# One pass over four tiles for the first unit's feed-forward, on weights still in SBUF; attention on four tokens at once

## The chip, the cores and the metric

The kernel runs on one core of one Trainium2 chip. The metric is the device time of one launch in microseconds (us), median of the runs. Names of the engines in the rows: PE is TensorE's matmuls, PEld its weight loads, DVE is VectorE, ACT is ScalarE, POOL is GpSimd, and SP is SyncE, which here issues all the transfers.

## The reference

2,048 tokens of 640 channels go through two layers of the same two blocks, with the same weights in both:

```python
def A(x):      # 32 heads of 20 channels, a window of 8 keys at distances 0, 2, ... 14
    q, k, v = split(layernorm(x) @ wqkv)               # 640 x 1920
    logits = sum(q * k[pos - 2*w], over 20 channels) * 20**-0.5    # masked where pos < 2*w
    return (softmax(logits, over the 8 keys) @ v[pos - 2*w]) @ wo
def B(x):      # per token, 640 -> 1536 -> 640
    return gelu(layernorm(x) @ w1 + b1) @ w2 + b2
x = x + A(x); x = x + B(layernorm(x)); x = x + A(x); x = x + B(layernorm(x))
```

## The kernel before, in words

The tokens are cut into four units of 512 (even and odd positions, two halves of each), and a unit into four tiles (`t`) of 128. A layer and a unit make a step `n` = 0 to 7. Matmuls run in float16 on operands that are split into a high part and the rest, three products for each (`PASS`), so every weight is also split once: ACT writes the scaled high part (L475), DVE the rest (L476).

For each step: `layernorm` ("a"), `qkv` (L648, in 16 pieces of 15 matmuls), whose results go through ACT (`ev`) to memory (`spill`), from which q, k and v come back with the window of the keys laid out (`fetch`, L690). `attention` works on DVE, for a quarter of the heads (a group `G`, 32 in all): products q by k (L732), their sums over 20 channels (L736), softmax (L741 to L751), weights by v (L758) and a tree of additions over the 8 keys (L766, L770). It takes the four tokens of a partition two at a time (`EH = 2`), so each of these instructions stands twice, with 2,560 elements per partition. The last group's rest (L780, on DVE) lets the DMA transposes go that feed `project` (L805, wo); then `layernorm` ("b") and DMA transposes (L620, `yT`).

`mlp` is the feed-forward. Its 12 blocks `e` each have inner matmuls (L871, weights `c1`, 15 of them), gelu and high part on ACT (L877, L880; `hhi`), the rest on DVE (L882; `hlo`) and outer matmuls (L892, weights `c2`; two passes need `hhi`, the third `hlo`). `PARTS` lists the passes: unit 0 of the first layer in two halves of two tiles (256 columns to an inner matmul), the next five steps in one pass of four tiles (512 columns); the last two steps are done together by `pair()`.

The weights of the feed-forward (24 blocks of 320 KB) are loaded to a staging buffer (L501), split, and the split pair is sent to memory (`mw`, L517); every pass of `mlp`, unit 0's too, loads its blocks from there (L864) into the slots `c1` and `c2`, three of each. Unit 0's first inner matmul waits until all 24 blocks and wo have been split (`split_done`).

The order on every engine is set ahead of time by `Plan.run`, which places the operations by priority in a modelled time and emits them; on the chip each engine takes its instructions in that order. SP's queue is such an order too: a transfer that waits holds all that stand behind it. DVE instructions named in `PAIRS` are those that share a port with POOL.

## Time and profile before

| | us |
|---|---|
| time, median of 3 runs (1144.21 to 1144.93) | 1144.45 |
| span of the profiled execution, first to last instruction | 1146.1 |
| PE's last matmul starts at | 1142.36 |
| PE busy | 1137.1 (99%) |
| DVE busy | 1038.4 (91%) |
| ACT busy | 606.6 (53%) |

The profiled execution has no time of its own beside its span; the span is 1.65 us above the median of the runs. A busy PE is one with a matmul in its pipe. Whether the matmuls also follow one another at full rate is seen from the starts in the timeline.

### The profile page before, as it was taken

The page shows a single profiled execution, that of the slowest core. Times are in us where ns is not written, and L with a number is a line of the kernel's source. Part 1 is how long each engine was busy: PE and PEld are TensorE (multiplying, and loading weights), DVE is VectorE, ACT ScalarE, POOL GpSimd, SP SyncE. Part 2 cuts the span into 40 slices and gives each one's busy share as a digit, 9 for nine tenths or more (in the row PEclk, how much of TensorE's full clock was granted, in tenths as well). Part 3 has the DMA queues.
Part 4 walks back from the last instruction along what each step waited for, and adds up shares of the span by engine and source line. Part 5 has one row for each costly group of instructions (what it writes and reads, how often), then busy time and mean ns, then how long its engine had stood idle before and what let it go on. Part 6 is the DMA issues. An engine that isn't in the chain of part 4 may idle for free.

```text
span 1146.1 us, 17470 instructions
## 1 busy us (share of the span) xinstructions
PE 1137.1 (99%) x6812; PEld 628.4 (55%) x6812; DVE 1038.4 (91%) x1028; ACT 606.6 (53%) x1131; POOL 113.2 (10%) x94
## 2 busy tenths in 40 slices
PE   9999999999999999999999999999999999999998
PEld 6444446567565465546555555556455556555476
DVE  7999999999899999999999999999999993847972
ACT  6485336536365275734537662479347445657720
POOL 1010000211111102110112012012111000000000
PEclk9999999999999999999999999999999999999999
DMA  9999998978976477576655965569686555974201
GB/s 318 307 299 266 329 302 244 321 264 244 239 189 232 140 221 213 178 207 198 186 187 176 221 190 164 175 188 192 164 247 183 175 171 156 217 239 122 65 24 69
DMA packets 239791, 235.47 MB, mean 205 GB/s; under 512 B 139020, under 2 KB 195164, under 8 KB 239708
## 3 DMA queue, kind: packets, MB, share of 16 engines
q1 hardware_dynamic: 239708, 234.36, 69.9%
q8 instruction: 53, 0.87, 0.3%
q14 instruction: 30, 0.25, 0.1%
HBM read 157.55 MB, written 44.78 MB: 177 GB/s over the span
## 4 chain that ended last, share of the span: by engine, by line
PE 72%; DVE 3%; DMA 1%; issue 0%; ACT 0%; DVEq 0%
PE acc L892 18%; PE ps L871 17%; PE ps L648 17%; PE ps L805 10%; PE acc L1073 4%; PE ps L1108 3%; PE ps L1073 2%; DMA yT<-w 1%; DVE yT L1020 1%; DVE pr L1005 1%; PE acc L1108 1%; DVE wq L1194 0%; DVE wq L1182 0%; DVE v L1195 0%; DVE xf L1196 0%
## 5 line engine op out<-in xcount | busy, mean ns | idle before, releaser
L648 PE MATMUL ps<-wq,yT 128*128 128x480 f16 (+1 forms) x1950 | 391.0, 363 | 1.5 <-DMA yT<-w 1.1
L648 PEld LDWEIGHTS <-yT 128*128 128x128 f16 x1950 | 189.3, 98 | 200.8 <-DMA yT<-w 1.4
L892 PE MATMUL acc<-c,act 128*128 128x512 f16 (+1 forms) x1728 | 249.3, 299 | 2.3 <-DMA c<-mw 1.6
L871 PE MATMUL ps<-yT,c 128*128 128x512 f16 (+1 forms) x1260 | 247.8, 350 | 0.0
L892 PEld LDWEIGHTS <-act 128*128 128x128 f16 x1728 | 136.1, 98 | 108.8 <-issue 1.9
L871 PEld LDWEIGHTS <-c 128*128 128x128 f16 x1260 | 120.9, 98 | 107.3 <-DMA c<-mw 0.3
L732 DVE TENSOR_TENSOR pr<-qk 128x2560 f32<-128x2560 f32 x64 | 179.5, 2808 | 0.0
L758 DVE TENSOR_TENSOR pr<-sm,v 128x2560 f32<-128x2560 f32 x64 | 179.1, 2818 | 0.3
L736 DVE TENSOR_REDUCE sm<-pr 128x128 f32<-128x2560 f32 x64 | 179.2, 2801 | 0.0
L665 ACT ACTIVATE ev<-ps 128x480 f32<-128x480 f32 x128 | 72.6, 568 | 177.2 <-PE ps L648 157.5
L877 ACT ACTIVATE act<-ps,b 128x512 f32<-128x512 f32 (+1 forms) x84 | 52.4, 624 | 172.9 <-PE ps L871 170.2
L766 DVE TENSOR_TENSOR pr<-pr 128x640 f32<-128x640 f32 (+1 forms) x128 | 143.1, 1150 | 0.3
L805 PE MATMUL ps<-wo,yT 128*128 128x320 f16 x960 | 131.7, 299 | 0.0
L805 PEld LDWEIGHTS <-yT 128*128 128x128 f16 x960 | 93.8, 98 | 37.4
L780 POOL TENSOR_TENSOR ohl<-w,ohl 128x640 f16<-128x640 f32 x24 | 34.9, 1456 | 425.9 <-DVE pr L732 171.6
L882 DVE TENSOR_TENSOR act<-act 128x512 f16<-128x512 f32 (+1 forms) x84 | 51.0, 609 | 16.0 <-ACT act L880 15.9
L587 POOL TENSOR_TENSOR ln<-ln,half 128x2 f32<-128x2 f32 (+1 forms) x31 | 36.2, 1173 | 276.6 <-ACT ln L584 276.6
L625 POOL TENSOR_TENSOR xf<-xf,b 128x640 f32<-128x640 f32 x24 | 37.3, 1558 | 144.6 <-DVE pr L732 58.4
L880 ACT ACTIVATE act<-act 128x512 f16<-128x512 f32 (+1 forms) x84 | 47.5, 565 | 3.4 <-PE acc L892 1.5
L610 ACT ACTIVATE w<-xf,ln 128x640 f32<-128x640 f32 x53 | 47.5, 909 | 2.7 <-DVE w L618 2.1
L570 ACT ACTIVATE junk<-xf 128x640 f16<-128x640 f32 x57 | 41.8, 733 | 12.9 <-DVE xf L814 8.0
L618 DVE TENSOR_TENSOR w<-w,w 128x640 f16<-128x640 f32 x56 | 45.7, 830 | 2.1 <-ACT w L616 2.1
(200 smaller groups left out, 984.1 us busy)
## 6 DMA issues: line engine op xcount, KB each, us to landing
c<-mw SPq DMA_DIRECT2D x174, 320.0 KB, 3.6
spill<-ev SPq DMA_DIRECT2D x64, 480.0 KB, 3.6
qk<-spill SPq DMA_DIRECT2D x32, 880.0 KB, 6.0
v<-spill SPq DMA_DIRECT2D x32, 880.0 KB, 5.3
qk<-spill SPq DMA_DIRECT2D x32, 320.0 KB, 3.6
act<-in_B_w_dram SPq DMA_DIRECT2D x24, 320.0 KB, 4.9
mw<-c SPq DMA_DIRECT2D x24, 320.0 KB, 4.7
pr<-in_B_w_dram SPq DMA_DIRECT2D x24, 320.0 KB, 4.1
```

The source lines that it names most:

```text
L648: nc.tensor.matmul(ps, transposed(yk)[:, a * KD + k, t * P:(t + 1) * P], wq[:, b, k, g, i0:i1], start=first and j == 0, stop=last and j == ...
L665: act(3 * GC, -400 + n, lambda i=i, pk=pk, ek=ek: nc.scalar.activation(tile_of(*ek)[:, :, i], tile_of(*pk)[:, :3 * GC].rearrange("p (a c) ...
L732: nc.vector.tensor_mul(tile_of(*pk), w[:, HALO + m + t0:HALO + m + t0 + EH, None, :].to_broadcast([P, EH, W, GC]), windows(w, t0, [GC, W], ...
L736: dve(E, G - 0.7, lambda pk=pk, t0=t0: nc.vector.tensor_reduce(lg(t0, t0 + EH).rearrange("p t w h -> p (t w h)"), tile_of(*pk).rearrange(" ...
L758: nc.vector.tensor_mul(tile_of(*vk).rearrange("p t w (h d) -> p t (w h) d", d=DH), lg(t0, t0 + EH).rearrange("p t w h -> p t (w h)")[:, :, ...
L766: dve(EH * w * GC, G - 0.9, lambda vk=vk, w=w: nc.vector.tensor_add(tile_of(*vk)[:, :, 0:w], tile_of(*vk)[:, :, 0:w], tile_of(*vk)[:, :, w ...
L805: nc.tensor.matmul(tile_of(*pk)[:, :D // 2], transposed(yk)[:, a * KD + k, t * P:(t + 1) * P], wo[:, b, k, c * D // 2:(c + 1) * D // 2], s ...
L871: nc.tensor.matmul(tile_of(*pk)[:, :nt], tile_of(*ck)[:, a, k * P:(k + 1) * P], transposed(yk)[:, c * KD + k, t0 * P:t1 * P], start=i == 0 ...
L877: act(nt, -430, lambda pk=pk, h32=h32, e=e: nc.scalar.activation(tile_of(*h32)[:, :nt], tile_of(*pk)[:, :nt], AF.Gelu_apprx_tanh, bias=b1[ ...
L882: dve(nt, -1000, lambda h32=h32, hk=hk: nc.vector.tensor_sub(tile_of(*hk)[:, 1, :nt], tile_of(*h32)[:, :nt], tile_of(*hk)[:, 0, :nt]), nee ...
L892: nc.tensor.matmul(accs[k][:, c0:c0 + n], tile_of(*hk)[:, a, (i - t0) * P:(i - t0 + 1) * P], tile_of(*wk)[:, c, w0:w0 + n], start=first, s ...
L1073: nc.tensor.matmul(tile_of(*to(i))[:, :HALF], hl()[:, a, i * P:(i + 1) * P], row(c), start=start and (a, c) == PASS[0], stop=(a, c) == PAS ...
```

## The change

Four things go together. `PARTS` gives unit 0 one pass over four tiles. That pass takes its weights from the slot in which the split wrote them (keys `("prep", e)`); the store to `mw` stays, for the later passes. The raw weights are loaded into slots of `c1` and `c2` too, so a raw block, its split pair and the blocks in use share three slots; the loads come where the pass needs them (priority -252, was 10), and no inner matmul waits for all splits. `attention` takes four tokens in one instruction (5,120 elements), and the logits lie with the 8 keys of a head next to each other (before, 8 heads apart). The first-layer `qkv` of unit 3 gets a late priority, so that it fills in.

```diff
-PARTS = [(0, 0, 2), (0, 2, 4)] + [(b, 0, 4) for b in range(1, 2 * NU - 2)]
+PARTS = [(b, 0, 4) for b in range(2 * NU - 2)]
...
     def prep_m(f, i, prio):
         ck = (f"c{i + 1}", ("prep", f))
...
-        prep_rows(("m", f, i), prio, src, lambda: tile_of(*ck)[:, 0], lambda: tile_of(*ck)[:, 1], [ck])
-        dma(328, prio - 5, lambda: nc.sync.dma_start(mw[i][f], tile_of(*ck)),
+        prep_rows(("m", f, i), (f"c{i + 1}", ("raw", f)), prio, src, lambda: tile_of(*ck)[:, 0], lambda: tile_of(*ck)[:, 1], [ck], -180)
+        dma(328, prio - 1, lambda: nc.sync.dma_start(mw[i][f], tile_of(*ck)),
...
-                prio, done = -500 + n + 0.01 * k, ("qkvp", n, t, g)
+                prio, done = (-500 if n != NU - 1 else 13) + n + 0.01 * k, ("qkvp", n, t, g)
...
-            dve(E, G - 0.6, qk, need=[("inq", G), ("ink", G)], give=[("qk", G, a)], use=[wk, pk, sk])
-            dve(E, G - 0.7, lambda pk=pk, t0=t0: nc.vector.tensor_reduce(
-                lg(t0, t0 + EH).rearrange("p t w h -> p (t w h)"), tile_of(*pk).rearrange("p t w (h d) -> p (t w h) d", d=DH),
-                axis=AX.X, op=OP.add), need=[("qk", G, a)], give=[("lg", G, a)], use=[pk, sk])
+        dve(E, G - 0.6, qk, need=[("inq", G), ("ink", G)], give=[("qk", G)], use=[wk, *pk, sk])
+        dve(E, G - 0.7, lambda: nc.vector.tensor_reduce(by_key(), heads(), axis=AX.X, op=OP.add),
+            need=[("qk", G)], give=[("lg", G)], use=[*pk, sk])
...
+        dve(E, G - 0.85, lambda: nc.vector.tensor_mul(
+            heads(), by_key()[:, :, :, None].to_broadcast([P, W, m * GH, DH]), windows(tile_of(*vw), [DH, m * GH], [1, DH])),
+            need=[("at", G), ("inv", G)], give=[("pv", G)], use=[vw, sk, *vk])
...
-            ck, wk = ("c1", j), ("c2", j)
-            for i, k in enumerate((ck, wk)):
+            ck, wk = (("c1", j), ("c2", j)) if at else (("c1", ("prep", e)), ("c2", ("prep", e)))
+            cgot, wgot = ([k] if at else [("lo", ("m", e, i))] for i, k in enumerate((ck, wk)))
+            for i, k in enumerate((ck, wk) if at else ()):
                 dma(328, -250 + j + 1.5 * i, lambda k=k, i=i, e=e: nc.sync.dma_start(tile_of(*k), mw[i][e]),
...
-            mm(3 * KD * nt, 15, j - 1.0 - AHEAD, inner, need=[*ready, ck, *split_done] + [("hhi", j - 2)] * (e > 1), give=[("hp", j)],
+            mm(3 * KD * nt, 15, j - 1.0 - AHEAD, inner, need=[*ready, *cgot] + [("hhi", j - 2)] * (e > 1), give=[("hp", j)],
...
-            prep_m(f, i, 10 + f)
+            prep_m(f, i, -252 + f)
```

Where it moves instructions, at three places. On PE, where unit 0's first inner matmuls end (`c_79` and `c_77` to `c_76` are slots of `c1`, `c_80` and `c_81` of `c2`, `yT_74` is unit 0's input). Before, the second block's inner matmuls are followed by outer ones:

```order
L871 MATMUL ps_95<-yT_74,c_79 128x256
L892 LDWEIGHTS act
L892 MATMUL acc_97<-c_81,act 128x512
...
L871 LDWEIGHTS c_80
L871 MATMUL ps_94<-yT_74,c_80 128x256
```

With the change the inner matmuls have 512 columns, and a piece of unit 3's `qkv` (15 matmuls) stands between them and the outer ones:

```order
L851 MATMUL ps_92<-yT_74,c_76 128x512
L639 LDWEIGHTS yT_72
L639 MATMUL ps_94<-wq,yT_72 128x480
...
L872 LDWEIGHTS act
L872 MATMUL acc_96<-c_80,act 128x512
```

All that stands ahead of it moved too: wo of unit 0 comes after 30 of unit 3's qkv matmuls (before, after 120), then 135 more of them, then the first inner matmuls. Of unit 3's last 75, 15 stand here and 60 after block 4's inner matmuls.

On DVE, around the second `hlo` of unit 0 (L882, now L862), before: two short instructions together, between attention's halves, and no split left to do:

```order
L758 TENSOR_TENSOR pr_77<-sm_90,v_68 128x2560
L882 TENSOR_TENSOR act<-act 128x256 x2
L766 TENSOR_TENSOR pr_77<-pr_77 128x2x640
L882 TENSOR_TENSOR act<-act 128x256
L766 TENSOR_TENSOR pr_77<-pr_77 128x2x320
```

With the change, from group 7's q by k on (L722); L466 is the split's rest, `c11<-c12` writes slot 1 of `c1` from the raw block in slot 2:

```order
L722 TENSOR_TENSOR pr_95<-qk0_67 128x5120
L862 TENSOR_TENSOR act_66<-act_66 128x512
L740 RECIPROCAL sm0_87<-sm0_87 128x32
L727 TENSOR_REDUCE sm1_88<-pr_95 128x8x32
L862 TENSOR_TENSOR act_66<-act_66 128x512
L466 SCALAR_TENSOR_TENSOR c11_77<-c12_78,c11_77 128x640
L466 SCALAR_TENSOR_TENSOR c21_80<-c22_81,c21_80 128x640
L466 SCALAR_TENSOR_TENSOR c12_78<-c10_76,c12_78 128x640
```

The splits of blocks 2 and 3 now stand behind the second `hlo`, between attention's long instructions; those of blocks 0 and 1 come much earlier, and blocks 4 to 11 follow in the same way.

On SP's queue, in the same stretch, before: loads of split blocks.

```order
L690 DMA v0_68<-spill00_135 128x1760
L864 DMA c22_83<-mw14_127 128x1280
L864 DMA c10_78<-mw06_117 128x1280
L864 DMA c11_79<-mw07_118 128x1280
L864 DMA c20_81<-mw15_128 128x1280
```

With the change: raw loads (L492) in turn with the stores of split blocks (L508), in one queue with attention's v (L681).

```order
L508 DMA mw03_113<-c12_78 128x1280
L492 DMA c10_76<-in_B_w1_dram 128x5x128
L681 DMA v0_68<-spill00_134 128x1760
L492 DMA c12_78<-in_B_w1_dram 128x5x128
L508 DMA mw13_125<-c20_79 128x1280
L492 DMA c22_81<-in_B_w2_dram 128x640
```

A raw load now waits until its slot's last reader is done, and the split of the block that it brings waits for the load.

## Rows read from the trace of the kernel before

**Rows 1.** Windows: length; busy us of PE, PEld, DVE, ACT, POOL; PEclk; DMA.

```profile
180.00:345.00 165.00, 161.58 (x1123) 104.61 (x1121) 158.64 (x147) 86.17 (x178) 22.67 (x16) 0.99 0.87 251
240.00:260.00 20.00, 20.00 (x153) 14.38 (x153) 19.17 (x17) 4.65 (x11) 2.43 (x2) 0.91 0.73 239
345.00:1140.00 795.00, 794.94 (x4722) 431.24 (x4721) 713.86 (x708) 423.74 (x770) 76.86 (x55) 1.00 0.61 176
```

**Rows 2.** Timeline of PE, 180 to 292: start, us, instruction, [idle before, releaser].

```profile
180.69 16.46 PE L805 MATMUL ps<-wo,yT 128*128 128x320 f16 x120
...
221.29 3.44 PE L871 MATMUL ps<-yT,c 128*128 128x256 f16 x30
...
237.99 0.72 PE L892 MATMUL acc<-c,act 128*128 128x512 f16 x4 [0.73 <-DVE act L882]
239.97 1.05 PE L892 MATMUL acc<-c,act 128*128 128x512 f16 x4 [1.26 <-DMA c<-mw]
240.81 3.16 PE L871 MATMUL ps<-yT,c 128*128 128x256 f16 x15
243.81 1.25 PE L892 MATMUL acc<-c,act 128*128 128x512 f16 x8
...
251.43 1.80 PE L871 MATMUL ps<-yT,c 128*128 128x256 f16 x15
253.07 1.79 PE L892 MATMUL acc<-c,act 128*128 128x512 f16 x12
...
289.52 0.70 PE L892 MATMUL acc<-c,act 128*128 128x512 f16 x4 [0.35 <-DMA c<-mw]
291.30 12.32 PE L648 MATMUL ps<-wq,yT 128*128 128x480 f16 x60 [1.07 <-DMA yT<-w]
```

**Rows 3.** The chain that ended last, in order of time: start, us, what.

```profile
303.62 16.30 PE ps L805 x120
319.92 12.15 PE ps L648 x60
...
399.73 3.26 PE acc L892 x24
402.99 3.24 PE ps L871 x15
```

**Rows 4.** Groups of instructions by line and form: count, busy us, mean ns of one.

```profile
L758 DVE TENSOR_TENSOR pr<-sm,v 128x2560 f32<-128x2560 f32 x64 | 179.1, 2818 | 0.3
L766 DVE TENSOR_TENSOR pr<-pr 128x1280 f32<-128x1280 f32 x64 | 93.8, 1483 | 0.1
L877 ACT ACTIVATE act<-ps,b 128x512 f32<-128x512 f32 x60 | 41.1, 685 | 137.6 <-PE ps L871 134.9 <-DVE pr L766 2.3
L749 DVE TENSOR_REDUCE sm<-sm 128x32 f32<-128x256 f32 x32 | 19.5, 611 | 6.3 <-ACT sm L747 6.2
L476 DVE SCALAR_TENSOR_TENSOR c<-act,c 128x640 f16<-128x640 f32 x24 | 19.1, 820 | 3.5 <-ACT c L475 3.5
L475 ACT ACTIVATE c<-act 128x640 f16<-128x640 f32 x24 | 16.8, 727 | 0.8 <-DMA act<-in_B_w_dram 0.8
L745 DVE TENSOR_TENSOR sm<-sm 128x256 f32<-128x256 f32 x32 | 13.4, 420 | 0.3
```

**Rows 5.** Timeline of DVE: start, us, instruction.

```profile
40.15 2.82 DVE L732 TENSOR_TENSOR pr<-qk 128x2560 f32<-128x2560 f32 x1
...
66.11 5.55 DVE L732 TENSOR_TENSOR pr<-qk 128x2560 f32<-128x2560 f32 x2
71.58 2.81 DVE L736 TENSOR_REDUCE sm<-pr 128x128 f32<-128x2560 f32 x1
...
226.02 0.76 DVE L882 TENSOR_TENSOR act<-act 128x256 f16<-128x256 f32 x2
```

**Rows 6.** Line L501 alone (weight loads): time to landing.

```profile
DMA to landing us min/median/max: 3.2/4.8/6.9
```

**Rows 7.** Line L587 alone (POOL's power in layernorm): duration ns min/median/max.

```profile
L587 POOL TENSOR_TENSOR ln<-ln,half x31: 547/706/3451, 12.8 to 980.6; 128x2 f32<-128x2 f32 x26, 128x1 f32<-128x1 f32 x5
```

More of the change, by code (lines that the diff above doesn't have):

```diff
@@ L356, in transposed @@
         return tile_of(*key).rearrange("p (k c) -> p k c", k=2 * KD)
-    blocks = [("o", k) for k in range(KD)] + [("m", f, i) for f in range(NF) for i in range(2)]
-    through = {name: next(pool for pool, n in THROUGH if i < n) for i, name in enumerate(blocks)}
-    split_done = [("lo", k) for k in blocks]
-    def passed(pool):
-        return [("lo", k) for k in blocks if through[k] == pool]
     wq = sb.tile([P, 2, KD, NG, 3, GC], HT, name="wq")
@@ L504, in prep_rows @@
             packet=4 * P if name[0] == "m" and not name[2] else 4 * D)
-        a, v = split(hi, lo, lambda: tile_of(*key))
-        act(D, prio, a, need=[("st", name)], give=[("hi", name)], use=[key, *use])
-        dve(D, next(p for n, p in LOP if blocks.index(name) < n), v, need=[("hi", name)], give=[("lo", name)], use=[key, *use])
+        a, v = split(hi, lo, raw)
+        act(D, prio + first, a, need=[("st", name)], give=[("hi", name)], use=[key, *use])
+        dve(D, LOP, v, need=[("hi", name)], give=[("lo", name)], use=[key, *use])
     def prep_o(k, prio):
-        prep_rows(("o", k), prio, lambda: A_wo[k * P:(k + 1) * P], lambda: wo[:, 0, k], lambda: wo[:, 1, k])
+        prep_rows(("o", k), ("sa", ("o", k)), prio, lambda: A_wo[k * P:(k + 1) * P], lambda: wo[:, 0, k], lambda: wo[:, 1, k])
     def prep_m(f, i, prio):
@@ L739, in attention, with heads, qk @@
-        last = [("lg", G, a) for a in range(NE)]
+        def heads():
+            return pr.rearrange("p w t (h d) -> p w (t h) d", d=DH)
+        pk, vk = ([("pr", (G, j, i)) for i in range(2)] for j in range(2))
+        def qk():
+            w = tile_of(*wk)
+            nc.vector.tensor_mul(pr.rearrange("p w t c -> p w (t c)"),
+                                 w[:, HALO + m:HALO + 2 * m].rearrange("p t c -> p (t c)")[:, None, :].to_broadcast([P, W, m * GC]),
+                                 windows(w, [1, m * GC]))
@@ L774, in hi @@
+        last = ("pv", G)
+        for w in (4, 2):
+            dve(m * w * GC, G - 0.9, lambda w=w: nc.vector.tensor_add(pr[:, 0:w], pr[:, 0:w], pr[:, w:2 * w]),
+                need=[last], give=[("ad", G, w)], use=vk)
+            last = ("ad", G, w)
+        dve(m * GC, G - 0.9, lambda: nc.vector.tensor_add(ot(), pr[:, 0], pr[:, 1]), need=[last], give=[("o", G)], use=[*vk, ok])
         def hi():
@@ L777, in attention @@
         act(m * GC, -350 + G, lambda: nc.scalar.activation(hi(), ot(), AF.Copy),
-            need=[("o", G, a) for a in range(NE)], give=[("oh", G)], use=[ok, hk])
+            need=[("o", G)], give=[("oh", G)], use=[ok, hk])
         def lo(eng):
@@ L782, in attention @@
         if g < NG - 1:
[L783 removed]
+            pool(ASIDE, -300 + G, lambda: lo(nc.gpsimd), need=[("oh", G), ("qk", G + 1)], give=[("ol", G)], use=[ok, hk],
                  pair=True)
```

88 lines of the change are left out of this document (30 added, 58 removed).

## The prediction

> **What bounds the kernel now.** I read the windows first. From 345 to 1140 us PE is busy for 794.94 of 795.00 us at the full granted clock [rows 1]; a stretch with a matmul in the pipe all the time can still hide slow matmuls, so the starts matter: in the chain, 24 outer matmuls take 3.26 us, 15 inner ones 3.24, 60 of qkv 12.15 and wo's 120 take 16.30, one behind the other, with PE before PE [rows 3]. There the kernel is a row of matmuls, and nothing that frees DVE, ACT or DMA moves the end. What can be won lies earlier: the window from 180 to 345 has 161.58 busy of 165.00, and 240 to 260 was granted 0.91 of the clock [rows 1]. PE's timeline shows the places [rows 2]: all four waits with a releaser lie between 237 and 292, which is unit 0's feed-forward. They are 0.73 us for its `hlo` on DVE, 1.26 and 0.35 for weights that come from memory, and 1.07 for the transposes of a layernorm ahead of qkv.
>
> **What the change removes.** (1) The four waits: 0.73 + 1.26 + 0.35 + 1.07 = 3.41 us. (2) Behind the first two the clock fell to its lower level, 1.2 GHz: the 15 inner matmuls from 240.81 to the next group at 243.81 took 3.00 us, while later 15 such took 253.07 - 251.43 = 1.64; the four outer ones ahead took 0.84 (239.97 to 240.81) where 24 take 3.26, so 0.54 [rows 2, 3]. That is 1.36 + 0.30 = 1.66. The wait of 1.07 at 291 had no such sequel. (3) Unit 0's inner matmuls: 24 groups of 15 with 256 columns at 1.64 against 12 groups with 512 at 3.24, 39.36 - 38.88 = 0.48 [rows 2, 3]. The columns are the same, the number of matmuls halves. All else on PE keeps its count. So 5.55 us can be won, and no more.
>
> **What it adds on PE: can the new pass be fed?** Its order has 90 fewer qkv matmuls ahead of unit 0's wo, 90 x 0.2025 = 18.2 us, so wo starts at 180.69 - 18.2 = 162.5. Then wo 16.3, 135 of qkv 27.3: the first inner matmul at 206.1 instead of 221.29. Two inner groups (6.5), 15 of qkv (3.0), the outer matmuls of block 0 (3.3) and the first two passes of block 1 (16 of 24, 2.2) bring PE to 221.1, where it wants the second `hlo`.
>
> On DVE the order has 98 instructions from the first q by k to that `hlo`. One of 2,560 elements takes 2.82 us and one of 1,280 takes 1.48 [rows 4], so 0.15 is fixed, and 5,120 make 5.49 alone; two of 2,560 start 5.47 apart together and overlap by 0.08 [rows 5], which makes 5.40 from start to start. So 22 long ones are 118.9, the six of 2,560 and six of 1,280 are 25.4, 25 of 640 at 0.75 are 18.9, 39 short ones at about 0.35 are 13.6: 176.8. The same sum for before, over the 144 instructions from 40.15 to the first `hlo` at 226.02, gives 179.2 where 185.9 passed [rows 5]: 6.7 idle, of which 3.5 were waits for ACT's part of the splits [rows 4], which the change puts elsewhere. One more split stands ahead of the first q by k (0.82). So 40.15 + 0.8 + 176.8 + 3.2 = 221.0, and the `hlo` is there at 221.7: PE waits 0.6, or 0 to 4 with none or all of the 6.7 idle and the unseen cost of the new layout.
>
> Next, block 4. Its raw load can go when block 3 is split, three splits behind that `hlo`, at 223.9. It lands after 4.8 (3.2 to 6.9) [rows 6], ACT takes 0.73, DVE 0.82 [rows 4], with 0.4 for issue and hand-over: 230.7, and a long instruction that has just begun on DVE adds up to 5.4. PE wants it at 222.5 + two inner groups 6.5 + outer matmuls 4.1 = 233.1. So 0 to 3 us late. The queue holds a store of a split block, attention's v and the next raw load behind one another; where the split is late, those are too, and v is what DVE asks for next.
>
> These delays don't add: PE that has waited once is later for all that follows, so the pass costs the largest delay, not their sum. I take 1.5 for it, nearer to the two estimates than to their ends, and 0.5 for the 1.07 before qkv, a chain of layernorm and transposes, which the change moves and doesn't remove: 2.0, with 0 and 6.5 as ends (4 for the `hlo`, 0.8 for a load at its longest beyond that, 1.7 for a second fall of the clock).
>
> **What it changes on DVE, at nothing.** Six pairs in each of 32 groups become one instruction: 192 x 0.15 = 29 us of busy time less. The sums over 8 keys read neighbours instead of elements 32 bytes apart: 0.61 us against 0.42 for a plain instruction of 256 [rows 4], 64 x 0.19 = 12 less. The stride moves into one long write and one long read, whose cost no row shows: 0 to 12 us in all. The cover is PE's unbroken row. What could uncover it is the longer instruction ahead of an `hlo`: from the end of an inner group to the third outer pass PE has 3.26 + 3.24 + 2.17 = 8.7 us of other work; gelu, high part and `hlo` take up to 0.69 each [rows 4], with hand-overs 2.4. That leaves 6.3, so one long instruction (5.4) hides, two don't. The 48 loads of split weights that go (24 blocks, two half passes) free DMA time that nothing waits for after 345.
>
> The port is a rule that speaks against long instructions. POOL's power in layernorm takes 0.55 us at the least and 3.45 at the most, one DVE instruction of 2,560 longer [rows 7]. The Trainium skill, "SBUF — State Buffer", section "SBUF: two separate sides", says that VectorE with two SBUF inputs and GpSimd hold a shared port for a whole instruction, and that the other one is fully blocked; by it the longest power here would be 6.1. The trace agrees as far as it goes. In this kernel the last tile of layernorm "b" of unit 0 would come 2.7 later by a power behind a long instruction and 2.7 by its own DVE step behind another, 5.4; between the end of wo and the first inner matmul there were 221.29 - (180.69 + 16.3) = 24.3 us [rows 2, 3] and are 27.3. So 2.4 late at worst.
>
> **The sum.** Against the profiled execution: 1146.1 - 3.41 - 1.66 - 0.48 + 2.0 = 1142.5 us of span, 3.6 less. That execution is 1.65 above the median of the runs, and 0.31% less of 1144.45 is 1140.9.
>
> **The rivals.** *New waits take the place of the old.* If `hlo` or the split blocks make PE wait for 3.3 to 7.9 us, the time is within 0.2% of before, which is about what a measurement of this kernel can tell. For it speaks that every block of the pass now hangs on a load, ACT, DVE and a slot in turn, and that two waits together brought the clock down before; against it, the filler of 75 qkv matmuls and wo of unit 1 among the blocks. About 1143.8. *POOL is held.* The layernorm 2.4 late: 1143.3. For it the longest row, against it the 3.0 us of added room. *The split's own cycle becomes the bound, and the kernel slower.* From inner block 2 to inner block 11 PE has nine inner groups (29.2), about as much of outer ones (28.6), 60 of qkv (12.2) and wo (16.3): 86.3 us, 9.6 for a block. A block's cycle is 4.8 + 0.73 + 0.82 + 0.4 = 6.75, and with a whole long DVE instruction in front each time 12.2: nine times 2.6 more, so 1144.45 - 5.5 + 23 = 1162. With half of one it is 9.4 and costs nothing; from 10.2 on it eats the gain, from 10.5 on it decides. Against it: a load may run while the block before it is in use, and the order puts two or three splits together. *Nothing is lost:* all waits go and none come, 1138.9.
>
> **How the numbers follow.** Forecast, new waits under 3.3 us (with the case of none, 0.12): 0.62, and all of it faster by more than 0.2%. New waits 0.15 and POOL 0.08: the same, 0.23. The cycle, with anything else that costs more than 7.9: 0.15, slower. The range goes from 1138.5 (nothing lost, and 0.4 for the runs' spread) to 1145.2 (waits of 6.3); about 0.05 lies below it and 0.14 above.
>
> **What will show it.** PE in the windows between 200 and 345: idle under 3 us, no stretch below the full clock, and inner groups of 512 at 3.24 in a row. The second `hlo` at 220 to 224, and PE's wait for it under 1 us. Waits for loads of `c` from `mw` gone in unit 0, at most one or two for L466. DVE near 1000 us busy, its long instructions at 5.4 to 5.5. The forecast is wrong if PE shows waits on split weights that return block after block, if the clock falls in the new pass, or if waits come up after 345, where there were none.

## The result, and the profile after

The changed kernel takes 1147.38 us (median of 10 runs, 1146.71 to 1148.25), the kernel before in the same sitting 1144.38 (10 runs, 1144.16 to 1146.83): a ratio of 1.0023, 95% interval 1.0014 to 1.0032. It is slower by about 0.2%; forecast were 1140.9 us, within 1138.5 to 1145.2.

The two traces seem to say the opposite: the changed kernel's span is 1145.2 us, and that of the first trace of before was 1146.1. Where a run's time and its span are both known, the time is 1.7 to 1.9 longer (here 1146.95 against 1145.2). So the first trace of before is of an execution that takes some 1147.9, longer than any of the ten runs of before; of all 128 runs of before on record three are as long (1148.32 to 1148.92). This decides half of the case, below.

The changed kernel's windows, with the columns of [rows 1]:

```profile
160.00:180.00 20.00, 18.53 (x131) 12.47 (x129) 19.93 (x11) 14.01 (x36) 1.14 (x2) 1.00 0.79 185
180.00:345.00 165.00, 162.67 (x941) 84.61 (x940) 162.36 (x121) 90.40 (x163) 28.63 (x18) 1.00 0.74 216
240.00:260.00 20.00, 20.00 (x103) 9.58 (x102) 19.74 (x13) 8.57 (x15) 1.69 (x1) 1.00 0.70 229
345.00:1140.00 795.00, 794.81 (x4702) 430.89 (x4701) 696.19 (x564) 413.72 (x755) 90.24 (x52) 1.00 0.61 173
```

From 345 us on PE is as busy as before. Up to there it idles 2.33 us between 180 and 345, and 1.47 ahead of 180, where before had no wait. DVE is busy for 162.36 of 165, which leaves it next to no room. The clock is full. PE's timeline, as in [rows 2]:

```profile
164.34 16.47 PE L784 MATMUL ps<-wo,yT 128*128 128x320 f16 x120 [1.47 <-DMA yT<-ohl]
...
207.98 6.64 PE L851 MATMUL ps<-yT,c 128*128 128x512 f16 x30
214.46 3.20 PE L639 MATMUL ps<-wq,yT 128*128 128x480 f16 x15
217.50 5.60 PE L872 MATMUL acc<-c,act 128*128 128x512 f16 x40
223.49 0.99 PE L872 MATMUL acc<-c,act 128*128 128x512 f16 x6 [0.40 <-DVE act L862]
224.32 6.64 PE L851 MATMUL ps<-yT,c 128*128 128x512 f16 x30
...
285.03 4.24 PE L784 MATMUL ps<-wo,yT 128*128 128x320 f16 x30 [0.18 <-DVE xf L793]
...
316.60 6.64 PE L851 MATMUL ps<-yT,c 128*128 128x512 f16 x30 [1.34 <-DMA yT<-w]
...
323.70 3.36 PE L872 MATMUL acc<-c,act 128*128 128x128 f16 x23 [0.41 <-DVE c L466]
```

Five waits, 3.80 us: wo of unit 0 for its transposes, the second `hlo`, wo of unit 1, unit 1's first inner matmul for the transposes of its layernorm, and the last block's split. After each wait some 0.17 us more are lost, in which the pipe fills: 30 inner matmuls in a row show 6.64 busy, but the next group starts 6.47 after their start.

Two stretches of other engines show what stands ahead of the first two waits. DVE where wo's input is finished (`ohl`, L759), and SP's queue beside it:

```profile
150.04 5.49 DVE L722 TENSOR_TENSOR pr<-qk 128x5120 f32<-128x5120 f32 x1
155.45 0.82 DVE L759 TENSOR_TENSOR ohl<-w,ohl 128x640 f16<-128x640 f32 x1
```

```profile
155.56 0.81 SPq L681 DMA_DIRECT2D qk<-spill  x2
156.48 9.91 SPq L772 DMA_TRANSPOSE yT<-ohl  x4
```

And DVE around the two `hlo` (L862), with ACT's high part (L860) that the second one needs:

```profile
211.15 5.48 DVE L722 TENSOR_TENSOR pr<-qk 128x5120 f32<-128x5120 f32 x1
216.55 0.68 DVE L862 TENSOR_TENSOR act<-act 128x512 f16<-128x512 f32 x1
217.15 0.35 DVE L740 RECIPROCAL sm<-sm 128x32 f32<-128x32 f32 x1
217.41 5.43 DVE L727 TENSOR_REDUCE sm<-pr 128x256 f32<-128x5120 f32 x1
222.76 0.68 DVE L862 TENSOR_TENSOR act<-act 128x512 f16<-128x512 f32 x1
223.35 2.44 DVE L466 SCALAR_TENSOR_TENSOR c<-c,c 128x640 f16<-128x640 f32 x3
```

```profile
215.57 0.63 ACT L860 ACTIVATE act<-act 128x512 f16<-128x512 f32 x1
```

ACT is done at 216.20, 1.2 us before DVE begins a 5.43-us sum, but in DVE's order the 0.68-us instruction stands behind that sum. The same at 150: ACT's high part of `ohl` is done at 150.78, and the rest of it runs behind the long q by k, 4.7 us later.

### The profile page after: what moved, and what is told of

It reads as the page before. It is cut to its first block, busy times and chain, and to the rows that moved or that the text cites. A ratio compares the mean times of both kernels' runs of the same rounds, so it can differ in the third digit from the quotient of the medians.

```text
span 1145.2 us, 16770 instructions
## 1 busy us (share of the span) xinstructions
PE 1135.2 (99%) x6632; PEld 609.9 (53%) x6632; DVE 1026.9 (90%) x823; ACT 600.3 (52%) x1107; POOL 140.2 (12%) x94
## 4 chain that ended last, share of the span: by engine, by line
PE 74%; DVE 19%; issue 5%; DMA 2%; ACT 1%; SPq 0%; DVEq 0%; ACTq 0%
PE ps L639 24%; PE acc L872 16%; PE ps L851 15%; PE ps L784 9%; DVE sm L727 4%; PE acc L1053 4%; PE ps L1088 3%; DVE pr L743 3%; DVE pr L748 3%; DVE pr L722 3%; PE ps L1053 2%; DMA b<-in_B_b_dram 1%; DVE pr L985 1%; DVE yT L1000 1%; DVE c L466 1%
## 5 line engine op out<-in xcount | busy, mean ns | idle before, releaser
L851 PE MATMUL ps<-yT,c 128*128 128x512 f16 x1080 | 243.4, 379 | 1.3 <-DMA yT<-w 1.3
L722 DVE TENSOR_TENSOR pr<-qk 128x5120 f32<-128x5120 f32 x32 | 175.4, 5480 | 21.0 <-DMA qk<-spill 20.7
L743 DVE TENSOR_TENSOR pr<-sm,v 128x5120 f32<-128x5120 f32 x32 | 177.7, 5554 | 0.4
L727 DVE TENSOR_REDUCE sm<-pr 128x256 f32<-128x5120 f32 x32 | 175.2, 5476 | 0.0
L851 PEld LDWEIGHTS <-c 128*128 128x128 f16 x1080 | 103.4, 98 | 122.2 <-issue 1.5
L748 DVE TENSOR_TENSOR pr<-pr 128x2560 f32<-128x2560 f32 x64 | 143.1, 2236 | 0.5
L857 ACT ACTIVATE act<-ps,b 128x512 f32<-128x512 f32 x72 | 49.2, 683 | 126.5 <-PE ps L851 126.2
L759 POOL TENSOR_TENSOR ohl<-w,ohl 128x640 f16<-128x640 f32 x24 | 48.6, 2026 | 346.4 <-DVE pr L743 151.8
L862 DVE TENSOR_TENSOR act<-act 128x512 f16<-128x512 f32 x72 | 49.8, 695 | 6.7 <-ACT act L860 6.5
L756 ACT ACTIVATE ohl<-w 128x640 f16<-128x640 f32 x32 | 23.5, 734 | 49.1 <-DVE w L751 49.0
L860 ACT ACTIVATE act<-act 128x512 f16<-128x512 f32 x72 | 45.0, 626 | 4.3 <-PE acc L872 2.9
```

Of the source, the lines that this page charges most:

```text
L722: nc.vector.tensor_mul(pr.rearrange("p w t c -> p w (t c)"), w[:, HALO + m:HALO + 2 * m].rearrange("p t c -> p (t c)")[:, None, :].to_broa ...
L727: dve(E, G - 0.7, lambda: nc.vector.tensor_reduce(by_key(), heads(), axis=AX.X, op=OP.add), need=[("qk", G)], give=[("lg", G)], use=[*pk, sk])
L743: dve(E, G - 0.85, lambda: nc.vector.tensor_mul(heads(), by_key()[:, :, :, None].to_broadcast([P, W, m * GH, DH]), windows(tile_of(*vw), [ ...
L748: dve(m * w * GC, G - 0.9, lambda w=w: nc.vector.tensor_add(pr[:, 0:w], pr[:, 0:w], pr[:, w:2 * w]), need=[last], give=[("ad", G, w)], use=vk)
L851: nc.tensor.matmul(tile_of(*pk)[:, :nt], tile_of(*ck)[:, a, k * P:(k + 1) * P], transposed(yk)[:, c * KD + k, t0 * P:t1 * P], start=i == 0 ...
L862: dve(nt, -1000, lambda h32=h32, hk=hk: nc.vector.tensor_sub(tile_of(*hk)[:, 1, :nt], tile_of(*h32)[:, :nt], tile_of(*hk)[:, 0, :nt]), nee ...
```

## The experiments

Times are medians, each with its ratio to runs of before on the same chip (95% interval). Before was itself 0.2 to 1.2 us longer in the later sittings, so the kernels are compared by ratio: 0.001 is 1.1 us, and the changed kernel has 1.0023. The letters (A, E, G and so on) are the theories named in the expected texts.

**1. The kernel before, again** (no edit).

> The kernel before, unchanged, for a second trace. Theory A (the execution shown in the first trace, 1146.1 us of span, was a slow one of its kind, and my sum was made against the wrong start): in the changed kernel every run is 1.75 us longer than its span (1146.95 against 1145.2), so an ordinary execution of before has a span of 1144.4 - 1.75 = 1142.6; this trace shows 1142.3 to 1143.2, with the clock at its full level between 240 and 260 and less than 2 us of waits in unit 0's feed-forward instead of 3.41. Rival B (that execution is ordinary, a profiled run of before is just longer than its timed ones): 1145.5 to 1146.5 again, with the same four waits and the fall of the clock. Time under both: ratio 1.000, within 0.001.

1144.96 us, 1.0003 (0.9995 to 1.0012); span 1143.2 for a run of 1144.96. PE's timeline has these waits and no others from 10 us on:

```profile
238.64 1.26 PE L892 MATMUL acc<-c,act 128*128 128x512 f16 x8 [0.69 <-DVE act L882]
...
269.70 3.20 PE L892 MATMUL acc<-c,act 128*128 128x128 f16 x23 [0.71 <-DVE xf L936]
...
288.42 12.32 PE L648 MATMUL ps<-wq,yT 128*128 128x480 f16 x60 [0.27 <-DMA yT<-w]
```

1.67 us instead of the 3.41 of [rows 2]; neither wait for weights from memory, and no fall of the clock (1.00 between 240 and 260). A holds. The first trace showed a real execution, but not an ordinary one: the 1.26-us wait for weights and the lower clock behind it are in that execution and not in this one.

From this trace the account closes. PE's last matmul starts at 1139.48 in it and at 1141.48 in the changed kernel, 2.00 later. The terms: waits 3.80 - 1.67 = 2.13; two more refills of the pipe, 0.34; fewer matmuls, -0.48; an earlier start (the first qkv of 480 columns at 16.89 instead of 17.31), -0.42; a late outer matmul at 619.40, 0.29. That is 1.86. It is the account of these two executions, whose times are 1.99 apart; the medians are 3.00 apart (2.6 by the ratio), and what the rest consists of no trace shows.

**2. Parts of the change alone.** Attention on four tokens in the kernel before; the changed kernel with attention on two; the changed kernel with unit 3's `qkv` early again. In each the planner makes a new order.

```diff
 # before_att4: before, with the changed kernel's attention(), one tile pr, and nothing else
+    pr = sb.tile([P, W, M, GC], FT, name="pr")
+    T["pr"] = [pr[:, i * W // 2:(i + 1) * W // 2] for i in range(2)]
 # after_att2: the changed kernel, with attention() of before (EH = 2) and its two tiles
+        "pr": many(sb, SLOTS["pr"], [P, EH, W, GC], FT, "pr"),
 # after_qkv_early
-                prio, done = (-500 if n != NU - 1 else 13) + n + 0.01 * k, ("qkvp", n, t, g)
+                prio, done = -500 + n + 0.01 * k, ("qkvp", n, t, g)
```

> Before, with attention on four tokens in one instruction and nothing else of the change. Theory A (the loss of the changed kernel comes from what its order does around wo and the feed-forward of units 0 and 1, not from the longer instructions): DVE some 15 to 30 us less busy, PE's row the same, time within 1 us of before (ratio 0.999 to 1.001). Rival C (the long instructions hold up hlo, layernorm and POOL, and that is the cost): 2 to 4 us slower (1.002 to 1.0035), with waits of PE for DVE or for transposes behind it between 160 and 345.

> The changed kernel with attention on two tokens at a time as before; one pass, weights from the split's slots and the late qkv stay. Theory A (the order around wo and the feed-forward costs it): still slower than before, 1145.5 to 1148 (ratio 1.001 to 1.003). Rival C (the long instructions cost it): at or under before, 1141 to 1144.4 (ratio 0.997 to 1.000).

> The changed kernel with unit 3's qkv of the first layer at its early priority again. wo of unit 0 keeps its place (30 qkv matmuls ahead of it), the first inner matmul goes back from 206 to 221 us, and nothing fills in between the blocks. Theory A (1.47 us of the loss is wo of unit 0 that now stands 18 us earlier and waits for its transposes): that wait of 1.2 to 2 us is still there; the hlo's wait of 0.40 and those for split blocks go, since the pass starts 15 us later and the splits are further; in all 1145 to 1147. Rival D (the late qkv is what tears unit 1's layernorm and wo apart and costs the most): 1143 to 1145, without the waits at 285 and 316. If without filler the pass waits for its weights block by block, 1148 or more.

Measured: 1154.64 (1.0087, 1.0073 to 1.0100), 1157.70 (1.0110, 1.0095 to 1.0126) and 1155.36 (1.0089, 1.0075 to 1.0103). No theory had that: each part alone costs 10 to 13 us. One wait of each timeline of PE, in this order:

```profile
255.64 1.25 PE L879 MATMUL acc<-c,act 128*128 128x512 f16 x4 [3.00 <-DVE act L869]
```

```profile
327.23 8.14 PE L864 MATMUL ps<-yT,c 128*128 128x512 f16 x30 [10.80 <-DVE pr L750]
```

```profile
244.06 1.76 PE L872 MATMUL acc<-c,act 128*128 128x512 f16 x6 [3.68 <-DVE c L466]
```

An `hlo` behind attention's instructions, unit 1's first inner matmul 10.80 us late, a split that the outer matmuls wait for, and in all three the clock below full in the windows read there (0.91, 0.89 and 0.83). What a part is worth by itself can't be read from these runs, since its order is made anew each time; what they show is that waits of 3 to 11 us come up in this stretch when the order changes.

**3. The order kept, DVE relieved.** q by k of groups 1 to 9 over four of eight keys.

```diff
...
+            wn = W // 2 if 0 < G < 10 else W
-            nc.vector.tensor_mul(pr.rearrange("p w t c -> p w (t c)"),
+            nc.vector.tensor_mul(pr[:, :wn].rearrange("p w t c -> p w (t c)"),
...
```

> The changed kernel with every instruction in its place, but the q by k of groups 1 to 9 forms four of the eight keys' products only (2,560 elements; the sums read what the tile held for the others), so that DVE has 9 x 2.7 = 24 us less to do up to 285 us. Theory E (in the changed kernel DVE is the engine that is late from 100 to 320 us, and PE's new waits, 1.47 for wo's transposes, 0.40 for hlo, 0.18 and 1.34 around unit 1's layernorm, 0.41 for a split, are its lateness seen at five places): they go, at 0.17 us of refilled pipe besides for each, so 1142.8 to 1144, under the time of before. Rival F (the waits are made by the queue of transfers and by ACT: transposes that take 1.3 to 4.4 us each to issue, raw loads of 4.8): 1146 or more, the wait at wo and that at 316 still there.

1146.10, 1.0005 (0.9996 to 1.0014): 2.1 us less than the changed kernel by the ratios (1.3 by the times), above E's time and at the lower end of F's. The trace is of the longest of its eleven runs (1146.88). Its waits from 10 us to 600:

```profile
176.28 4.24 PE L785 MATMUL ps<-wo,yT 128*128 128x320 f16 x30 [1.07 <-ACT ps L797]
...
322.48 3.37 PE L873 MATMUL acc<-c,act 128*128 128x128 f16 x23 [1.91 <-DVE c L466]
...
397.92 16.46 PE L785 MATMUL ps<-wo,yT 128*128 128x320 f16 x120 [0.74 <-ACT ps L797]
```

The waits at 164, 223, 285 and 316 are gone, the two that F names among them, so they were DVE's. But others that stood just behind them come up: ACT's copies of the residual to PSUM (L796, here L797), and the last block's split on DVE.

```profile
320.42 2.01 DVE L466 SCALAR_TENSOR_TENSOR c<-c,c 128x640 f16<-128x640 f32 x1
```

ACT's part of that split is done at 316.49; DVE, relieved only up to 285 us, comes to it 3.9 us later, behind two of attention's instructions, and takes 2.01 us for it instead of 0.82 (experiment 8 shows why). E named the places rightly and was wrong that DVE's load is all there is: PE's waits from 10 us to 600 are still 3.72 us, 1.81 of them for ACT, though 24 us less on DVE gave back most of the loss by the ratios (0.0018 of 0.0023; by the times 1.3 of 3.0).

**4. The order kept, four operations moved.** `behind(a, b)` puts operation `a` directly behind `b` in the emitted order:

```diff
+    behind(("ol", 3), ("oh", 3))            # the rest of ohl, ahead of the long q by k
+    behind(("qk", 4), ("ol", 3))
+    behind(("inq", 5), ("oT", 0, 1))        # two transposes ahead of the next q and k
+    behind(("ink", 5), ("inq", 5))
```

> The changed kernel with its order kept but for four operations: the rest of unit 0's last group (the 0.82 us on DVE that lets the transposes go) stands ahead of the next group's long q by k instead of behind it, and two of the four transposes ahead of the next loads of q and k. DVE waits some 0.9 us for ACT there, the transposes start 4 us earlier. Theory E (DVE's chain to the hlo sets the place, and a wait ahead of it is only the same lateness seen early): the wait of 1.47 at wo goes, and the wait for the second hlo grows from 0.40 to 2 to 3; time the same or up to 1 us longer, 1147 to 1148.4. Rival G (the wait at wo is a loss of its own): 1.6 us less, 1145.5 to 1146.

1148.40, 1.0031 (1.0019 to 1.0042). wo waited 1.46 all the same, now for ACT's copy (L796), which stands behind the exponential of the next group; the second `hlo` waited 1.34 instead of 0.40, since DVE had idled 0.8 us for ACT. That idling delayed ACT's copies too: they start at 163.74 in this run, and in the changed kernel 0.8 us earlier:

```profile
162.94 0.78 ACT L796 ACTIVATE ps<-xf 128x320 f32<-128x320 f32 x2
```

A single copy takes 0.44, so in the changed kernel the copies alone would have held wo, which PE wanted at 162.87, for some 0.5 us. The next run takes this cause away as well:

```diff
+    for c in (1, 0):
+        behind(("xw", 0, 0, c), ("ev", 3, 0, 0))   # L796 ahead of the exponential
```

> The run with the four moved operations, and on ACT the first two copies of the residual to PSUM (L796, which wo's matmuls add to) stand ahead of the exponential (L737) instead of behind it, for in that run they, not the transposes, were what wo waited for (1.46 us). All else in its place. Theory E (up to the second hlo it is DVE's chain that sets the time; a wait ahead of it is the same lateness seen early): wo waits under 0.5 us, the wait for the second hlo grows from 1.34 to 2.4 to 3, time within 0.7 us of that run's 1148.4. Rival G (the wait at wo is a loss of its own): 1.4 us less than that run, the hlo's wait unchanged.

1149.81, 1.0039 (1.0025 to 1.0052). wo's first matmuls no longer wait; PE's timeline where the `hlo` is due, and the window with its clock (PE busy, clock, DMA):

```profile
216.45 5.70 PE L872 MATMUL acc<-c,act 128*128 128x512 f16 x40 [0.24 <-ACT act L860]
224.91 1.78 PE L872 MATMUL acc<-c,act 128*128 128x512 f16 x6 [2.77 <-DVE act L862]
226.49 7.29 PE L851 MATMUL ps<-yT,c 128*128 128x512 f16 x30
```

```profile
220.00:230.00 10.00, 7.23 (x36) 0.83 0.84 266
```

The wait has moved, not gone: 1.47 + 0.40 = 1.87 in the changed kernel, 2.80 after the first edit, 0.21 + 0.24 + 2.77 = 3.22 now. It has grown because the edits cost DVE time as well: it idles 0.80 for ACT and, in the second run, 0.62 for q and k, whose loads now stand behind two transposes, and the second `hlo` ends at 224.85 instead of 223.44. E holds and G falls: what PE gained at wo it waited for at the `hlo`. The 1.4 us over the first edit's time (0.9 by the ratios) are as much as the clock cost in this trace: it fell behind the long wait (0.83), 6 outer matmuls took 1.78 instead of 0.99 and 30 inner ones 7.29 instead of 6.64.

**5. ACT's part of the splits first**, alone and with the moves.

```diff
-        prep_rows(("m", f, i), (f"c{i + 1}", ("raw", f)), prio, src, ..., [ck], -180)
+        prep_rows(("m", f, i), (f"c{i + 1}", ("raw", f)), prio, src, ..., [ck], -260)
```

> The changed kernel with one number changed: ACT's part of a split goes ahead of all else that ACT has ready (offset -260 instead of -180). The order up to the first inner matmul at 206 us is nearly the same; behind it splits come sooner, and of unit 3's last 75 qkv matmuls one piece each stands between the blocks, two of them where PE waited for unit 1's layernorm. Theory E with H (up to the hlo it is DVE's lateness, 2.2 us; the 2.5 us around 285 to 324 are the order's, since the filler was used up by 253): 1.47 and 0.40 stay, the waits at 285 to 324 go; 1144.5 to 1146. Rival I (the time of unit 1's layernorm is set by DVE too, so waits of the same size come back at other places): 1146.5 to 1148.

> Both edits: ACT's part of a split first, and the four operations moved. Theory E: as the run with the first edit alone, or up to 1 us longer. Rival G: 1.6 us less than with the first edit alone, and under the time of before if that one is within 1 us of it.

> ACT's part of a split first, the four moved operations, and L796 ahead of the exponential. Theory E: as the runs with the first edit, 1145.2 to 1146.2, with the second hlo's wait at 2 to 3 us in place of wo's. Rival G: 1.4 us less, 1144 to 1144.6.

1145.62 (1.0004, 0.9995 to 1.0013), 1145.81 (1.0003, 0.9994 to 1.0012) and 1147.95 (1.0023, 1.0014 to 1.0032). The first has one wait between 10 and 600 us, for wo (2.51); those at 285, 316 and 323 are gone, and pieces of unit 3's `qkv`, the filler, now stand between the blocks up to 312. So E with H holds, but for the 0.40 at the `hlo`, which went while wo's wait grew: some 2 us of the loss were the filler's, which the changed kernel had used up by 253 us. Freeing wo again brings nothing: the second kernel waits 1.43 at wo and 1.34 for the `hlo`, the third 2.77 for the `hlo`. G falls twice more. No kernel here is under the time of before; the first two are level with it, some 2 us below the changed kernel by the ratios. The third is 2 us over E's time, and its trace, of a shorter run (1146.59), doesn't show why. The mean granted clocks of its runs point to the clock: 1.000 in the two shortest (1145.55 and 1146.59), 0.998 or 0.999 in the nine others, where 0.001 of the span is 1.1 us.

**6. A piece of filler earlier**, on the first kernel of 5: the planner is given a longer `hlo` for block 1.

```diff
-                need=[("hhi", j)], give=[("hlo", j)], use=[h32, hk])
+                need=[("hhi", j)], give=[("hlo", j)], use=[h32, hk], more=1.5 * (j == 1))
```

> ACT's part of a split first, and the planner is told that the second hlo takes 1.5 us longer than it does, so that it puts a piece of unit 3's qkv (15 matmuls, 3.05 us) between the first passes of block 1 and its third pass, which needs that hlo; fewer are left for the blocks behind. Theory E: no wait for the second hlo; wo waits 1.5 to 2.5 us as before, and what was gained there comes back as a wait of 1 to 3 us at unit 1's first inner matmul, around 317, whose layernorm DVE and ACT also set: 1145 to 1147. Rival R (the filler was all that lacked, and unit 1's layernorm has room): no wait there, 1143.5 to 1144.5, under the time of before.

1150.22, 1.0041 (1.0027 to 1.0055). No wait for the `hlo`, and 1.19 at wo; but

```profile
321.10 11.56 PE L851 MATMUL ps<-yT,c 128*128 128x512 f16 x45 [2.49 <-issue]
398.51 16.47 PE L784 MATMUL ps<-wo,yT 128*128 128x320 f16 x120 [1.27 <-DMA yT<-ohl]
```

The lateness comes back at unit 1's first inner matmul, as E had it ("issue": the profile names no releaser; the last of unit 1's transposes was issued at 316.39), and again at the next wo; E's time was 3 us too low, partly for the clock (45 inner matmuls in 11.56 us, which take 9.88 later in the changed kernel). R falls.

**7. The second `hlo` directly behind the first**, in four kernels. DVE's order, the changed kernel's against the first of them:

```diff
-L862 TENSOR_TENSOR act<-act 128x512
-L740 RECIPROCAL sm_87<-sm_87 128x32
-L727 TENSOR_REDUCE sm_88<-pr 128x8x32
-L862 TENSOR_TENSOR act<-act 128x512
+L862 TENSOR_TENSOR act<-act 128x512 x2
+L740 RECIPROCAL sm_87<-sm_87 128x32
+L727 TENSOR_REDUCE sm_88<-pr 128x8x32
 L466 SCALAR_TENSOR_TENSOR c_77<-c_78,c_77 128x640
```

> The changed kernel with one thing moved on DVE: the second hlo (0.68 us) stands directly behind the first, ahead of a reciprocal and of the 5.43-us sum of a group (L727), not behind them. ACT had its input done at 216.2 us, the hlo ran at 222.76. Theory S (the wait for the second hlo comes from that place alone): the wait of 0.4 to 1.2 for it is gone, nothing comes in its place, 0.6 to 1.2 us less than the changed kernel, 1146.0 to 1146.9. Rival E (DVE's whole chain is the bound up to unit 1's layernorm): the hlo's wait goes, the one at 316 grows by as much, 1147 to 1147.8.

> ACT's part of a split first and the second hlo directly behind the first; wo still waits for its transposes. Theory S: the wait at wo (1.5 to 2.5) stays, for the hlo none, 1144.6 to 1145.6, that is 0 to 1 us less than with the first edit alone. Rival E: the same time as with the first edit alone, 1145.4 to 1146.2.

> The run in which neither the transposes nor the copies to PSUM hold wo (1149.8, with 2.77 us of wait for the second hlo and 1.4 us at the lower clock behind it), and the second hlo directly behind the first. Theory S: no wait over 0.3 us from 160 to 285, no fall of the clock; 4.4 us less, 1145 to 1146, if unit 1's layernorm has the room. Rival E: the same up to 285, and then a wait of 3 to 4 us for unit 1's transposes around 316, 1147.5 to 1148.5.

> ACT's part of a split first, the moves that free wo, and the second hlo directly behind the first. Theory S: the 2.77 and 0.24 us of the same kernel with the hlo in its old place go and nothing comes back, 1142.6 to 1144.2: under the time of before. Rival E: 1 to 3 us come back at unit 1's first inner matmul between 312 and 317, 1144.5 to 1147.

1149.05 (1.0031, 1.0019 to 1.0042), 1146.51 (1.0011, 1.0002 to 1.0020), 1149.29 (1.0035, 1.0021 to 1.0049) and 1147.27 (1.0014, 1.0005 to 1.0023). No gain that is clear of the noise: by the ratios to the same kernels without the move, the first two are 0.9 and 0.8 us longer, the other two 0.5 and 1.0 shorter. In the first of them PE, DVE and POOL read:

```profile
226.07 6.22 PE L851 MATMUL ps<-yT,c 128*128 128x512 f16 x28 [1.49 <-DVE c L466]
```

```profile
217.19 2.49 DVE L862 TENSOR_TENSOR act<-act 128x512 f16<-128x512 f32 x2
```

```profile
217.45 1.69 POOL L759 TENSOR_TENSOR ohl<-w,ohl 128x640 f16<-128x640 f32 x1 [18.61 <-DVE pr L722]
```

What PE wants next, the split of the following block, stood behind the same sum (L466 at 223.35 in the changed kernel), and now PE waits for it, 2 us on, in all four kernels (1.29 to 1.65). E expected the loss of the first kernel to come back at 316; it came back at 226. But the edit did something else as well: the pair takes 2.49 us where two single ones take 0.68 each, because POOL's rest of `ohl` starts 0.26 us behind it. In the changed kernel POOL's instruction began at 216.80, and ran mostly beside the reciprocal and the sum, which took its usual 5.43. So the edit paid for its gain with 1.2 us of DVE, and S can't be judged by these four alone; experiment 9 takes that away.

**8. POOL held back.** One POOL instruction, `ohl`'s rest for the next unit, waits for a later `hlo`.

```diff
+    rest, lo = find[("ol", 8)], find[("hlo", 12)]
+    rest["behind"] = lo
...
```

> The changed kernel in its order, but one POOL instruction (the rest of a group's output, L759, which ran from 319.07 to 322.96 us) waits until the hlo of the thirteenth block is done. Theory P (that instruction and DVE held each other up: it took 3.89 us where others of its line take 1.4, and DVE's split L466 behind it took 2.02 where others take 0.82, which is what PE waited for at 323.70): the split takes 0.82 again, PE's wait of 0.41 for it goes, 0.4 to 0.6 us less in the trace, 1146.6 to 1147.4 in time. Rival Q (the split of 2.02 is long for another reason, its load or ACT): it still takes 2, and the wait stays.

1146.85, 1.0015 (1.0007 to 1.0024); against the changed kernel's 1.0023 that settles nothing in time, but the rows do. The changed kernel, DVE and then POOL:

```profile
318.88 2.83 DVE L748 TENSOR_TENSOR pr<-pr 128x2560 f32<-128x2560 f32 x1
321.62 2.02 DVE L466 SCALAR_TENSOR_TENSOR c<-c,c 128x640 f16<-128x640 f32 x1
```

```profile
319.07 3.89 POOL L759 TENSOR_TENSOR ohl<-w,ohl 128x640 f16<-128x640 f32 x1 [20.16 <-DVE pr L743]
```

With POOL held back the split is as short as all the others, and PE's wait for it is gone:

```profile
323.11 0.82 DVE L466 SCALAR_TENSOR_TENSOR c<-c,c 128x640 f16<-128x640 f32 x1
```

P holds. (From the `hlo` on, both engines are 1.5 us later here than in the changed kernel, so the wait did not go because PE was late.) POOL's instruction, 1.40 us at its shortest, first waited out the DVE instruction that had started 0.19 us ahead of it, and then the split waited out POOL's.

**9. Experiment 7 without the collision.** POOL's rest of `ohl` comes behind the reciprocal that follows the pair, on the second and the fourth kernel of 7.

```diff
+    find[("ol", 5)]["behind"] = find[("rc", 6)]
+    behind(("ol", 5), ("rc", 6))
```

> ACT's part of a split first, the second hlo directly behind the first, and POOL's instruction that ran into the two (the rest of a group's output, L759) held back until the reciprocal behind them, so that POOL runs beside the sum L727 as it did before the hlo was moved. In the four runs with the moved hlo the pair took 2.48 us instead of 1.29, and all behind it came 1.2 us later. Theory T (POOL's collision, not DVE's chain, ate what the move brings): the pair takes 1.3, the wait for the split of the next block falls from 1.29 to 0.2 or none, 1 to 1.4 us less than without the hold (1146.5, ratio 1.0011): ratio 0.9995 to 1.0003. Rival E (DVE's chain to the split is as late without POOL): the split's wait stays over 0.8 us, ratio 1.0007 or more.

> The same hold in the kernel in which wo waits for nothing. Theory T: the waits of 1.72 for the hlo and 1.65 for the split fall to about 0.5 each, 2 to 2.5 us less than without the hold (1147.3, ratio 1.0014): ratio 0.9990 to 0.9998, under the time of before. Rival E: one of the two waits stays at 1.2 us or more, or one of that size comes up before 345 us; ratio 1.0004 or more.

1145.34 (1.0000, 0.9991 to 1.0009) and 1146.00 (1.0005, 0.9996 to 1.0013), where 7 had 1.0011 and 1.0014. DVE of the first, and PE of the first and of the second:

```profile
219.53 1.29 DVE L862 TENSOR_TENSOR act<-act 128x512 f16<-128x512 f32 x2
```

```profile
227.21 6.22 PE L851 MATMUL ps<-yT,c 128*128 128x512 f16 x28 [0.25 <-DVE c L466]
```

```profile
219.28 4.25 PE L872 MATMUL acc<-c,act 128*128 128x512 f16 x30 [0.52 <-DVE act L862]
...
225.61 6.22 PE L851 MATMUL ps<-yT,c 128*128 128x512 f16 x28 [1.65 <-DVE c L466]
```

The pair is at 1.29 again, and the wait for the split falls from 1.29 to 0.25 where wo still waits: T holds there, and the collision was worth some 1 us of experiment 7 (1.04 in this wait, 1.3 by the ratios, whose intervals overlap). (The profiled execution was a longer one, 1148.02, with 2.58 at wo and both engines some 2.5 us late from there; set against 7's second kernel, PE's outer matmuls begin 2.52 later, the split only 1.47.) With wo freed the wait for the `hlo` falls from 1.72 to 0.52, but the split is waited for as before, 1.65; the kernel is 1.0 us under experiment 7's by the ratios and not under before: E holds there. The split can't be put in front of the sum either as things stand: ACT's part of it starts at 220.57, behind PE's outer matmuls that free its slot, and the sum has begun at 219.40. So S's gain is too small to be told from nothing (1.0004 without the moved `hlo` in experiment 5, 1.0000 with it), and no version is under the time of before: the best three are level with it (1.0000, 1.0003, 1.0004).

## Why the prediction was wrong, point by point

**The start of the sum** failed first, and by most: "1146.1 - 3.41 - 1.66 - 0.48 + 2.0", carried over to the median in proportion. The 1.65 us between that execution's span and the median of the runs were noted and taken for an offset; with the 1.75 by which a time exceeds its span, that execution was 3.4 us longer than an ordinary one, of which its waits (3.41 instead of 1.67) and its clock (1.66) make up all. An ordinary execution of before has 1.67 us of waits where the first trace has 3.41, and no fall of the clock where 1.66 were counted. So of the 5.55 us that "can be won" some 2.7 were there (1.67, three refills of 0.17, for which the sum had no term, and 0.48). On the ordinary span of 1143.2 the same plan of gains and losses comes out within 0.2 us of no change.

**"So wo starts at 180.69 - 18.2 = 162.5."** PE was there at 162.7, but wo could not start before 164.3. The step moved wo by the matmuls ahead of it and didn't ask for its input: DVE's rest of `ohl` moved only from 170.19 to 155.45, 14.7 us, and the slack between it and wo shrank from 10.5 to 7.3 us, of which a first transpose that lands 7.8 us after its issue takes all. Without the transposes ACT's copies to PSUM would still have held it for some 0.5 (experiment 4). Missing term: 1.47.

**The second `hlo`** was placed well: 221.7 forecast for its end, 223.4 measured; "PE waits 0.6" against 0.40, which is right only because PE itself was late by wo's wait. Experiment 4 shows the two to be one lateness (1.87 us here, 2.80 and 3.22 with wo's causes taken away at DVE's expense), so the sentence "These delays don't add" holds up to here.

**The split's cycle** did not decide. Block 4's split came in time, and in the whole pass PE waited for one split, 0.41 us, and that for POOL. In the orders of experiment 2 it does become a wait (3.68 for L466): the mechanism is real, but it did not bound this order.

**"0.5 for the 1.07 before qkv"** failed in size: unit 1's wo and layernorm wait 0.18 and 1.34. The filler of 75 `qkv` matmuls, named against the rivals, was used up by 253 us; experiment 5 shows these waits to be gone with the filler spread to 312. New waits in all: 3.80 for the 2.0 taken, and 0.17 more behind each; this is the second step that failed, and with the start it makes up most of the miss.

**DVE, "29 us of busy time less" and 12 for the keys.** The layout part was right, and the stride that it moves elsewhere costs nothing: the sums over keys take 25.8 us instead of 39.1, and the multiply that reads with the stride (L743) has the same median as q by k, 5.484. The fixed parts gave 14.8 instead of 29 (the five lines of products, sums and tree: 713.4 to 698.6 in the second trace of before and here). The 0.15 per pair was the wrong row to take: by the prediction's own 5.47 for two against 5.40 for one, joining a pair saves 0.07 from start to start, and 192 x 0.07 is 13. All in all DVE is busy for 1026.9 us, against 1038.2 in that trace; "near 1000" was forecast. Some went to POOL, as the groups by form show, to compare with [rows 4]:

```profile
L743 DVE TENSOR_TENSOR pr<-sm,v 128x5120 f32<-128x5120 f32 x32 | 177.7, 5554 | 0.4
L722 DVE TENSOR_TENSOR pr<-qk 128x5120 f32<-128x5120 f32 x32 | 175.4, 5480 | 21.0 <-DMA qk<-spill 20.7
L748 DVE TENSOR_TENSOR pr<-pr 128x2560 f32<-128x2560 f32 x32 | 92.6, 2893 | 0.3
L739 DVE TENSOR_REDUCE sm<-sm 128x32 f32<-128x256 f32 x32 | 13.0, 410 | 1.6 <-ACT sm L737 1.5
```

L748 takes 2893 ns on the mean where 2,560 elements took 2818, and the longest 4025: it runs from 246.84 on, and POOL's L759 had begun at 246.49.

**POOL.** The rival had it make unit 0's layernorm late; it didn't. POOL's power now takes up to 4.74 us, against 3.45 [rows 7]:

```profile
L578 POOL TENSOR_TENSOR ln<-ln,half x31: 548/1210/4741, 13.2 to 981.3; 128x2 f32<-128x2 f32 x26, 128x1 f32<-128x1 f32 x5
```

But the price fell on a split instead, and by way of DVE waiting for POOL, the side that the working left out. The Trainium skill, "SBUF — State Buffer", section "SBUF: two separate sides", says that of a VectorE instruction with two SBUF inputs and a GpSimd one that reads SBUF, whichever starts first keeps the shared port for its whole instruction, and the other is fully blocked. Experiments 7 to 9 agree in both directions: POOL took 3.89 us where 1.40 is its shortest, a split 2.02 where 0.82 is usual, and two `hlo` 2.49 where 1.29 is usual.

**What was forecast rightly:** under 3 us of idle PE between 200 and 345 (2.33), no stretch below the full clock, inner groups of 512 at 3.24, no wait for weights from memory, one wait for a split, none over 0.3 us behind 345. Every sign that was to show the change at work came but DVE's busy time; the sum was wrong all the same, because its start and its new waits were. The rival that came nearest is the first: new waits in place of the old, which from an ordinary start end a little slower than before.

## What to carry to other kernels

A trace is one execution: before its waits are counted as winnable, hold its span against the times of the runs, with the constant that lies between a run's time and its span (1.75 here), and if it stands off the median by as much as the change is to win, take a second trace. When a stage is moved earlier on the bound engine, go through everything that feeds it again; the wait that was hidden by its old place is the first thing to come up. And where a fixed order meets an engine that is 98% busy, a wait is that engine's lateness showing at the first place that can: taking it away there moves it to the next, as the waits of experiments 4 and 6 did. How late it can be is set by what stands ahead in the order: here a 0.68-us instruction waited behind one of 5.43.
